# The last chunk's gate cut into thirds, and small idle matmuls in the first routing round

## The chip, the cores and the metric

The kernel runs on one NeuronCore of a Trainium2 chip. The time of a run is the device time of one execution in microseconds; "before" is the median of six executions. A profile comes from one further execution, with its own time and its own span from the first to the last instruction.

## What is computed

A gated linear recurrence (four batches, eight heads, 768 steps, head size 48) gives x, 3072 tokens of 384 numbers. Then a mixture of eight experts with balanced assignment: all token and expert pairs are gone through by falling logit, and a pair is taken when the token is still free and the expert has fewer than 384 tokens.

```python
for t in range(S):
    state = f[:, :, t, :, None] * state + np.einsum('bhd,bhe->bhde', k[:, :, t], v[:, :, t])
    y[:, :, t] = np.einsum('bhd,bhde->bhe', q[:, :, t], state)
...
logits = x @ w_gate                       # 3072 x 8
order = np.argsort(-logits.flatten())
for idx in order:
    tok, e = (int(idx) // E, int(idx) % E)
    if assigned[tok] >= 0 or counts[e] >= cap:
        continue
    assigned[tok] = e
    counts[e] += 1
...
for e in range(E):
    mask = assigned == e
    h = np.maximum(x[mask] @ w1[e], 0.0)  # 384 x 1024
    out[mask] = h @ w2[e]                 # 1024 x 384
```

## The kernel before

**Attention.** The 24 chunks (128 steps of one batch each) go through a pipeline of six stages; `attention(first, last)` runs its steps. In each step the parts of FILLING, FULL or LAST (lines 403 to 415) are issued in that order, each for the chunk whose stage is due. PE, DVE, ACT and POOL run what they are given in exactly the order in which the program issues it (`manual_schedule`), and SP issues loads. The last steps use LAST, in which only the end of the last chunks is left.

The end of a chunk: `values` and `queries` make x in two PSUM banks, which are copied to SBUF (line 355; for the last chunk one by ACT, one by DVE) and stored to DRAM by a DMA on ACT's queue. One step later `transposed` (line 360) turns x by three 128x128 transposes into one PSUM bank X, `x_copy` (367) copies X to xT on DVE in one instruction, `gate` (371) multiplies xT with the gate's weights, three blocks of 128 rows for each of two token halves, into columns D to D+E of the same bank, and `to_logits` (383) copies the result into `logits`.

Small pieces of DVE work for the routing are kept in the deque `small` and issued in the part `beside`: two in a step, one in a step of LAST. Six are queued before the last five steps: the five of `part(0, NCH - 1)` (line 670: row maximum `best`, `choice`, keys `over`, `masked`, `pick`) and `at_steps(0, NCH - 1)` (679), which compares the keys of 20 of the 24 columns with the first digit's 16 thresholds into `above`. The last four columns come with the last chunks and are done after the pipeline (lines 1176 to 1179). In the last step `counts_so_far` (379) calls `counted` (687): 20 small matmuls that count the tokens of those 20 columns over each threshold, and a DVE subtraction into `need`, what is still wanted.

**Routing.** `assign_and_run` finds the experts in rounds. Each round searches, for every expert, a threshold by five digits of 16 steps. In the first round (and two digits of the second) this is `digit_alone` (759): for each 8 columns DVE compares keys to thresholds (`reached`), PE adds the counts of the columns in 128x8 matmuls (24, or 4 for the first digit, whose other 20 are in `need`), DVE compares (`fills`) and reduces (`filled`), and one tiny matmul with `unit` gives the digit to all partitions, which the next digit's compare reads. Later rounds use `digit_beside` with expert matmuls from `pe_work` placed between. `assign` (842) counts the tokens over the found level (`sums`, a matmul with `ones`), marks them and lowers `places`.

Then `expert_list` numbers the tokens of the expert that is full: `index` loads the expert's number to SP, which starts the load of w1; `tokens` has POOL gather the rows of x in three indirect DMAs and starts the load of w2. `ffn` gives the expert's pieces to `pe_work`: three turns (transposes of gathered rows), 24 up matmuls, 24 down matmuls. In the first round `pe_work` is empty.

**Idle matmuls.** `idle_turns(n, nothing)` (124) issues n matmuls of `ones` (128x128) with `idle` (128x384, both BF16) into a bank that nobody reads. There are 19 and 12 at the start, three and a few more in the pipeline, one between the pieces of the first expert list (line 1126), 13 behind it (1133), and two in each of the second round's first two digits (776).

PSUM has eight banks: in attention six in turn under the tag "bank" and two under "sum", later three "r", three "H", one "O" (in which idle matmuls write) and `last_O`.

Of the kernel before, what the change touches and what calls it, by code (L numbers as in the profile page):

```python
# [26 lines left out]
def kernel(  # L27
# [60 lines left out]
    def ps(name, tag="bank"):  # L88
        return banks.tile([128, 512], FP32, name=name, tag=tag, bufs=BANKS[tag])
# [31 lines left out]
    k_bufs = [kept([128, H, DP], FP32, f"kg{i}") for i in range(NB)]  # L121
    a_bufs = [kept([128, 2, HP, 128], FP32, f"am{i}") for i in range(NB)]

    def idle_turns(n, nothing):

        for _ in range(n):
            nc.tensor.matmul(out=nothing[:, 0:CAP], lhsT=ones[:], rhs=idle[:], start=True,  # L127
                             stop=True)

    def constants():  # L130
# [209 lines left out]
    def queries(G):  # L340
        b, c, Y = G["b"], G["c"], G["Y"]
        G["x"] = x = work.tile([128, D], FP32, name="x", tag="x", bufs=3)
        if G["R"] is not None:
            for hp in range(HP):
                for j in range(2):
                    for par in range(2):
                        rows = slice(DP * par, DP * par + DH)
                        nc.tensor.matmul(
                            out=Y[par][HC * j:HC * j + HC, DH * hp:DH * hp + DH],
                            lhsT=G["qT"][rows, hp, HC * j:HC * j + HC],  # L350
                            rhs=G["R"][rows, hp, :],
                            start=False, stop=True, skip_group_check=True)
        for par in range(2):
            copy = nc.vector.tensor_copy if par and G["i"] == len(chunks) - 1 else nc.scalar.copy
            copy(out=x[:].rearrange("t (a r d) -> t r a d", r=2, d=DH)[:, par],
                 in_=Y[par][:, 0:HP * DH].rearrange("t (a d) -> t a d", d=DH))
        row = S * b + C * c
        nc.scalar.dma_start(out=xd[row:row + C, :], in_=x[:])

    def transposed(G):  # L360
        X = ps("X")
        for d in range(DC):
            nc.tensor.transpose(out=X[:, 128 * d:128 * d + 128],
                                in_=G["x"][:, 128 * d:128 * d + 128], identity=ident[:])
        G["X"] = X

    def x_copy(G, work=work):
        G["xT"] = work.tile([128, DC, 128], FP32, name="xT", tag="xT")
        nc.vector.tensor_copy(out=G["xT"][:].rearrange("p c t -> p (c t)"), in_=G["X"][:, 0:D])

    def gate(G):
        X = G["X"]
        for d in range(DC):
            for j in range(2):
                half = slice(HC * j, HC * j + HC)
                nc.tensor.matmul(out=X[half, D:D + E], lhsT=G["xT"][:, d, half], rhs=wg[:, d, :],
                                 start=(d == 0), stop=(d == DC - 1))

    def counts_so_far(G):
        if G["i"] == len(chunks) - 1:  # L380
            begun[3]()

    def to_logits(G, to=None):
        if to is None:
            to = logits[:, G["b"] * NCH + G["c"]]
        nc.vector.tensor_copy(out=to, in_=G["X"][:, D:D + E])

    chunks = [{"b": b, "c": c, "i": c * B + b} for c in range(NCH) for b in range(B)]
    AHEAD = 2
# [2 lines left out]
    def beside(G):  # L392
# [18 lines left out]
            (q_columns, 2), (k_columns, 2), (k_last, 2), (beside, 0), (clamp, -1), (queries, 4),  # L411
            (scores, 3))
    LAST = ((scores, 3),) + FIRST + ((x_copy, 5), (k_copy, 2), (values, 4), (queries, 4),
                                     (counts_so_far, 5), (gate, 5), (to_logits, 5),
                                     (beside, 5))

    small, small_pe = deque(), deque()
# [1 line left out]
    def attention(first, last):  # L419
        for step in range(first, last):  # L420
            if step + AHEAD < len(chunks):
                load(chunks[step + AHEAD])
            for part, stage in (FILLING if step < STAGES else
                                FULL if step < len(chunks) + 2 else LAST):
                if 0 <= step - stage < len(chunks):
                    part(chunks[step - stage])
                if part is sums and small_pe:
                    small_pe.popleft()()
                if part is beside:
                    for _ in range(min(len(small), 1 if step >= len(chunks) + 2 else 2)):  # L430
                        small.popleft()()

    for G in chunks[0:AHEAD]:
# [99 lines left out]
    def by_e(t):  # L533

        return t[:].rearrange("p c e -> p e c")
# [104 lines left out]
    def begin():  # L640

        nc.vector.memset(places[:], float(CAP))
        nc.vector.memset(wanted[:], float(CAP))
        nc.vector.memset(penalty[:], 0.0)
        nc.vector.tensor_copy(out=left[:], in_=first[:])
        nc.vector.memset(taken[:], 0.0)
        nc.vector.memset(lowest[:], 0.0)
        choice, over, pick = rt([NT, E], "choice", BF16), rt([NT], "over"), rt([NT], "pick")
        above = rt([NT, NTH], "above", BF16)
        need = rt([E], "need", FP32, 1)  # L650

        def part(c0, c1):
            n = c1 - c0

            def of(t):
                return t[:].rearrange("p (b c) -> p b c", b=B)[:, :, c0:c1]

            def of_e(t):
                return t[:].rearrange("p (b c) e -> p b c e", b=B)[:, :, c0:c1]

            def over_e(t):
                return t.unsqueeze(3).to_broadcast((128, B, n, E))

            best = rt([B, n], "best0")
            masked = rt([B, n, E], "masked0", BF16)

            def keys():
                level_keys(best[:], of(over))

            return [  # L670
                lambda: reduce(best[:], of_e(logits), ALU.max),

                lambda: tt(of_e(choice), of_e(logits), over_e(best[:]), ALU.is_equal),
                keys,
                lambda: tt(masked[:], of_e(choice), first[:].unsqueeze(1).unsqueeze(1).to_broadcast(
                    (128, B, n, E)), ALU.mult),
                lambda: reduce(of(pick), masked[:], ALU.max)]

        def at_steps(c0, c1):

            n = c1 - c0
            tt(above[:].rearrange("p (b c) t -> p b c t", b=B)[:, :, c0:c1],
               over[:].rearrange("p (b c) -> p b c", b=B)[:, :, c0:c1].unsqueeze(3).to_broadcast(
                   (128, B, n, NTH)),
               digits[0][0][:].unsqueeze(1).unsqueeze(1).to_broadcast((128, B, n, NTH)), ALU.is_ge)

        def counted():

            r = ps("counted")
            cols = [c for c in range(NT) if c % NCH < NCH - 1]  # L690
            for c in cols:
                nc.tensor.matmul(out=r[0:NTH, 0:E], lhsT=above[:, c, :], rhs=choice[:, c, :],
                                 start=(c == cols[0]), stop=(c == cols[-1]))
            tt(need[0:NTH, :], wanted[0:NTH, :], r[0:NTH, 0:E], ALU.subtract)

        return (choice, over, pick, counted, above, need), part, at_steps

    def assign_and_run(begun=None, also=None, again=None, exact=None):
# [60 lines left out]
        def digit_alone(above, parts, choice, unit, counted=None, turns=(0, 0)):  # L759

            some(pe_work, turns[0])
            r = bank("cnt", "r")
            cols = [c for c in range(NT) if not counted or c % NCH == NCH - 1]
            for c in cols:
                if c % 8 == 0 and not counted:
                    parts(c, c + 8)
                nc.tensor.matmul(out=r[0:NTH, 0:E], lhsT=above[:, c, :], rhs=choice[:, c, :],
                                 start=(c == cols[0]), stop=(c == cols[-1]))
            fills = rt([E], "fills")
            tt(fills[0:NTH, :], r[0:NTH, 0:E], counted[1][0:NTH, :] if counted else  # L770
               wanted[0:NTH, :], ALU.is_ge)
            filled = rt([1], "filled", BF16)
            reduce(filled[0:NTH, :], fills[0:NTH, :], ALU.max)
            if turns[1]:
                some(pe_work, turns[1])
                idle_turns(2, bank("nothing", "O"))
            digit = r[:, 128:129]
            nc.tensor.matmul(out=digit, lhsT=unit[0:NTH, :], rhs=filled[0:NTH, :], start=True,
                             stop=True)
            return digit, ALU.add  # L780
# [61 lines left out]
        def assign(choice, over, pick, slots):  # L842
# [4 lines left out]
            count = rt([E], "count", BF16)  # L847
            with nc.allow_low_precision("counts of at most 24"):
                reduce(count[:], by_e(sure), ALU.add)
            some(pe_work, slots[0])  # L850
            r = bank("sums", "r")
            nc.tensor.matmul(out=r[:, 0:E], lhsT=ones[:], rhs=count[:], start=True, stop=True)
# [323 lines left out]
    for n, piece in enumerate(part(NCH - 1, NCH)):  # L1176
        piece()
        if n == 2:
            at_steps(NCH - 1, NCH)
    in_order.__exit__(None, None, None)  # L1180
    attn.close()

# [150 lines left out]
```

## Time and profile before

| | us |
|---|---|
| median of six executions | 459.4 (458.15 to 462.03) |
| the profiled execution, its own time | 460.21 |
| its span | 458.4 |
| PE busy in the span | 437.4 (95%) |
| DVE busy | 265.7 (58%) |
| ACT busy | 139.3 (30%) |
| POOL busy | 135.5 (30%) |
| expert matmuls on PE, up (L1054, x384) and down (L1066, x192 and x192) | 132.6 + 67.0 + 66.7 |
| 74 idle matmuls, L127, PE | 19.4 |
| mean granted TensorE clock | 0.98 of full |

A line of the timeline gives start and length in us, the engine (PE a matmul, PEld its weight load, DVE, ACT, POOL, SP), the kernel's line, the operation, what it writes and reads, shapes, how many, and in brackets the idle time before and who ended it. The busy time of a matmul contains its way through the array, so a chain of matmuls issued 0.025 apart shows 0.17 for each.

### The profile page before, as it was taken

The numbers are of one execution on the slowest core, as the hardware profiler recorded it, in microseconds if no ns is written. First come the engines' busy times: TensorE is split into PE (matmuls) and PEld (weight loads), VectorE is DVE, ScalarE is ACT, GpSimd is POOL, SyncE is SP. The second block draws the span as 40 slices with busy tenths as digits, with TensorE's granted clock in tenths as the row PEclk, the third lists the DMA queues.
The fourth block names the chain that finished last, engine by engine and source line by source line (L and its number), as shares of the span: only waits on it lengthen the run. The fifth ranks groups of instructions, "written<-read, shape, count | busy, mean of one in ns | idle before, by whom it ended". The sixth has DMA issues, their size and how long they took to land. (4 is left out here: it accounts for less than half of the span.)

```text
span 458.4 us, 11902 instructions
## 1 busy us (share of the span) xinstructions
PE 437.4 (95%) x4893; PEld 293.8 (64%) x4893; DVE 265.7 (58%) x878; ACT 139.3 (30%) x322; POOL 135.5 (30%) x189
## 2 busy tenths in 40 slices
PE   8999999999999669999999999999999999999994
PEld 5788888888888535565565565565565565556552
DVE  5779977678987686647547647647637636000000
ACT  4566665566652001202212212212212212212210
POOL 1556655555551012032032033023023025101001
PEclk9999999999999859999999999999999999999999
DMA  9999998989511127082082072082082087400001
GB/s 156 184 200 206 195 190 188 192 182 181 122 38 37 37 68 261 0 305 75 6 294 80 8 287 85 2 292 75 13 292 70 17 292 242 175 19 34 0 19 39
DMA packets 118399, 59.11 MB, mean 129 GB/s; under 512 B 101664, under 2 KB 112960, under 8 KB 118336
## 3 DMA queue, kind: packets, MB, share of 16 engines
q1 hardware_dynamic: 111760, 44.06, 38.6%
q0 software_dynamic: 3072, 9.44, 6.3%
q10 hardware_dynamic: 3504, 4.77, 3.0%
q8 instruction: 40, 0.66, 0.6%
q14 instruction: 23, 0.19, 0.1%
HBM read 48.77 MB, written 9.49 MB: 127 GB/s over the span
## 5 line engine op out<-in xcount | busy, mean ns | idle before, releaser
L1054 PE MATMUL H<-xeT,w 128*128 128x384 f32 x384 | 132.6, 496 | 0.1
L1054 PEld LDWEIGHTS H<-xeT,w 128*128 128x128 f32 x384 | 69.1, 190 | 45.7 <-issue 4.0
L1066 PE MATMUL O<-w,hT 128*128 128x384 f32 x192 | 67.0, 491 | 0.0
L1066 PE MATMUL last_O<-w,hT 128*128 128x384 f32 x192 | 66.7, 491 | 0.0
L1058 ACT ACTIVATE hT<-H 128x384 f32<-128x384 f32 x64 | 31.4, 491 | 101.3 <-PE H L1054 85.3
L1066 PEld LDWEIGHTS last_O<-w,hT 128*128 128x128 f32 x192 | 35.1, 190 | 22.8 <-issue 1.9
L1066 PEld LDWEIGHTS O<-w,hT 128*128 128x128 f32 x192 | 34.9, 190 | 21.5 <-issue 1.3
L1071 POOL DMA_INDIRECT out_dram<-o,token x21 | 21.2, 1011 | 83.6 <-ACT o L1070 83.3
L324 DVE COPY_PREDICATED am<-mask,A 128x512 f32<-128x512 int32 x48 | 32.3, 727 | 18.2 <-PE A L319 18.2
L971 POOL TENSOR_TENSOR block<-past 128x72 f32<-128x72 f32 x8 | 2.4, 300 | 112.1 <-DVE at L551 100.1
L190 POOL TENSOR_TENSOR low<-g,upper 128x384 fp32r<-128x384 f32 x22 | 22.2, 1011 | 44.7 <-DVE upper L188 41.1
L1046 ACT COPY xeT<-Xe 128x384 f32<-128x384 f32 x24 | 11.4, 480 | 58.0 <-PE Xe L1043 57.7
L334 PE MATMUL Y<-v,am 128*64 128x48 f32 x768 | 27.5, 223 | 0.8 <-DVE am L324 0.8
L319 PE MATMUL A<-qT,kT 48*64 48x128 f32 x768 | 27.0, 273 | 1.0 <-issue 1.0
L334 PEld LDWEIGHTS Y<-v,am 128*64 128x64 f32 x768 | 24.8, 138 | 1.7 <-DVE am L324 1.3
L1013 POOL DMA_INDIRECT xe<-xd,token x21 | 21.4, 1021 | 10.9 <-DVE full L548 4.4
L243 POOL TENSOR_TENSOR kg<-k,ek 128x384 f32<-128x384 f32 x23 | 23.1, 1003 | 2.2 <-ACT ek L221 2.2
L319 PEld LDWEIGHTS A<-qT,kT 48*64 48x64 f32 x768 | 21.4, 133 | 2.1 <-issue 2.0
L220 ACT ACTIVATE eq<-dl 128x384 f32<-128x384 f32 x24 | 12.6, 523 | 30.2 <-DVE dl L218 30.2
L127 PE MATMUL nothing<-idle,ones 128*128 128x384 bf16 x74 | 19.4, 400 | 1.6 <-DVE ones L132 1.5
L1070 ACT COPY o<-O 128x384 f32<-128x384 f32 x12 | 5.8, 479 | 40.7 <-PE O L1066 40.7
L237 DVE TENSOR_TENSOR qg<-q,eq 128x384 f32<-128x384 f32 x24 | 17.4, 723 | 0.6 <-ACT eq L220 0.6
(223 smaller groups left out, 659.5 us busy)
## 6 DMA issues: line engine op xcount, KB each, us to landing
w<-in_moe_w_dram SPq DMA_DIRECT2D x16, 1536.0 KB, 7.1
f<-in_f_logit_dram SPq DMA_DIRECT2D x24, 192.0 KB, 4.8
q<-in_q_dram SPq DMA_DIRECT2D x24, 192.0 KB, 4.6
k<-in_k_dram SPq DMA_DIRECT2D x24, 192.0 KB, 4.7
v<-in_v_dram SPq DMA_DIRECT2D x24, 192.0 KB, 4.6
xd<-x ACTq DMA_DIRECT2D x24, 192.0 KB, 3.0
xe<-xd,token POOLq DMA_INDIRECT x21, 3.1
out_dram<-o,token POOLq DMA_INDIRECT x21, 2.6
```

The source lines that it names most:

```text
L127: nc.tensor.matmul(out=nothing[:, 0:CAP], lhsT=ones[:], rhs=idle[:], start=True, stop=True)
L190: nc.gpsimd.tensor_tensor(out=low[:], in0=g[:, :, 0:DH], in1=upper[:].bitcast(FP32), op=ALU.subtract)
L237: nc.vector.tensor_tensor(out=G["qg"][:, :, 0:DH], in0=G["q"][:], in1=G["eq"][:], op=ALU.mult)
L243: engine.tensor_tensor(out=G["kg"][:, :, 0:DH], in0=G["k"][:], in1=G["ek"][:], op=ALU.mult)
L319: nc.tensor.matmul(out=A[par][HC * j:HC * j + HC, 128 * hp:128 * hp + 128], lhsT=G["kT"][rows, hp, HC * j:HC * j + HC], rhs=G["qT"][rows, ...
L324: nc.vector.copy_predicated(am[:, par], mask[:].unsqueeze(1).to_broadcast((128, HP, 128)), A[par][:].rearrange("s (a t) -> s a t", t=128))
L334: nc.tensor.matmul(out=Y[par][HC * j:HC * j + HC, DH * hp:DH * hp + DH], lhsT=G["am"][:, par, hp, HC * j:HC * j + HC], rhs=G["v"][:, 2 * h ...
L1013: nc.gpsimd.indirect_dma_start(out=xe[:], out_offset=None, in_=xd[:, :], in_offset=bass.IndirectOffsetOnAxis(ap=token[:, i:i + 1], axis=0))
L1054: nc.tensor.matmul(out=L["H"][:, 0:CAP], lhsT=L["w1"][:, d, 128 * ft:128 * ft + 128], rhs=xT[:, d, :], start=(d == 0), stop=(d == DC - 1))
L1058: nc.scalar.activation(out=hT[:, ft, :], in_=L["H"][:, 0:CAP], func=AF.Relu)
L1066: nc.tensor.matmul(out=L["O"][:, 0:D], lhsT=hT[:, ft, 128 * i:128 * i + 128], rhs=L["w2"][:, ft, :], start=(ft == 0), stop=(ft == FC - 1))
L1071: nc.gpsimd.indirect_dma_start(out=outs[next(tiles)][:, :], out_offset=bass.IndirectOffsetOnAxis(ap=L["token"][:, i:i + 1], axis=0), in_=o ...
```

## The change

The gate of the last chunk gets a PSUM bank for each transpose and one for its result, and a copy for each third, the middle one on ACT. The counts so far move behind the gate and its logits; their subtraction moves behind the last `at_steps`. `small` gives two pieces in each step, also in LAST. `idle_turns` takes a size, and in `digit_alone` without turns of its own 12 (first digit) or 6 (others) idle matmuls of 128 columns stand ahead of the counts and 4 ahead of the digit's product; 12 stand ahead of the sums in `assign` when there is no expert work.

```diff
-    def idle_turns(n, nothing):
+    def idle_turns(n, nothing, size=CAP):
 
         for _ in range(n):
-            nc.tensor.matmul(out=nothing[:, 0:CAP], lhsT=ones[:], rhs=idle[:], start=True,
+            nc.tensor.matmul(out=nothing[:, 0:size], lhsT=ones[:], rhs=idle[:, 0:size], start=True,
                              stop=True)
...
+    def last(G):
+        return G.get("i") == len(chunks) - 1
+
     def transposed(G):
-        X = ps("X")
+
+        G["X"] = X = [ps("X") for _ in range(DC)] if last(G) else [ps("X")] * DC
         for d in range(DC):
-            nc.tensor.transpose(out=X[:, 128 * d:128 * d + 128],
+            nc.tensor.transpose(out=X[d][:, 128 * d:128 * d + 128],
                                 in_=G["x"][:, 128 * d:128 * d + 128], identity=ident[:])
-        G["X"] = X
 
     def x_copy(G, work=work):
-        G["xT"] = work.tile([128, DC, 128], FP32, name="xT", tag="xT")
-        nc.vector.tensor_copy(out=G["xT"][:].rearrange("p c t -> p (c t)"), in_=G["X"][:, 0:D])
+        if last(G):
+            G["xT"] = [work.tile([128, 128], FP32, name="xTd", tag="xTd", bufs=DC)
+                       for _ in range(DC)]
+            for d, t in enumerate(G["xT"]):
+                copy = nc.scalar.copy if d == 1 else nc.vector.tensor_copy
+                copy(out=t[:], in_=G["X"][d][:, 128 * d:128 * d + 128])
+        else:
+            xT = work.tile([128, DC, 128], FP32, name="xT", tag="xT")
+            nc.vector.tensor_copy(out=xT[:].rearrange("p c t -> p (c t)"), in_=G["X"][0][:, 0:D])
+            G["xT"] = [xT[:, d, :] for d in range(DC)]
 
     def gate(G):
-        X = G["X"]
+        G["lg"] = lg = ps("lg") if last(G) else G["X"][0]
         for d in range(DC):
             for j in range(2):
                 half = slice(HC * j, HC * j + HC)
-                nc.tensor.matmul(out=X[half, D:D + E], lhsT=G["xT"][:, d, half], rhs=wg[:, d, :],
+                nc.tensor.matmul(out=lg[half, D:D + E], lhsT=G["xT"][d][:, half], rhs=wg[:, d, :],
                                  start=(d == 0), stop=(d == DC - 1))
 
     def counts_so_far(G):
-        if G["i"] == len(chunks) - 1:
-            begun[3]()
+        if last(G):
+            G["need"] = begun[3]()
...
-                                     (counts_so_far, 5), (gate, 5), (to_logits, 5),
+                                     (gate, 5), (to_logits, 5), (counts_so_far, 5),
                                      (beside, 5))
...
                 if part is beside:
-                    for _ in range(min(len(small), 1 if step >= len(chunks) + 2 else 2)):
+                    for _ in range(min(len(small), 2)):
                         small.popleft()()
...
-            tt(need[0:NTH, :], wanted[0:NTH, :], r[0:NTH, 0:E], ALU.subtract)
+            return lambda: tt(need[0:NTH, :], wanted[0:NTH, :], r[0:NTH, 0:E], ALU.subtract)
...
             cols = [c for c in range(NT) if not counted or c % NCH == NCH - 1]
+            if not turns[1]:
+                idle_turns(12 if counted else 6, bank("nothing", "O"), 128)
             for c in cols:
...
                 idle_turns(2, bank("nothing", "O"))
+            else:
+                idle_turns(4, bank("nothing", "O"), 128)
             digit = r[:, 128:129]
...
                 reduce(count[:], by_e(sure), ALU.add)
+            if not pe_work:
+                idle_turns(12, bank("nothing", "O"), 128)
             some(pe_work, slots[0])
...
         if n == 2:
             at_steps(NCH - 1, NCH)
+            chunks[-1]["need"]()
```

More of the change, by code (lines that the diff above doesn't have):

```diff
@@ L353, in queries @@
         for par in range(2):
-            copy = nc.vector.tensor_copy if par and G["i"] == len(chunks) - 1 else nc.scalar.copy
+            copy = nc.vector.tensor_copy if par and last(G) else nc.scalar.copy
             copy(out=x[:].rearrange("t (a r d) -> t r a d", r=2, d=DH)[:, par],
@@ L385, in to_logits @@
             to = logits[:, G["b"] * NCH + G["c"]]
-        nc.vector.tensor_copy(out=to, in_=G["X"][:, D:D + E])
+        nc.vector.tensor_copy(out=to, in_=G["lg"][:, D:D + E])
     chunks = [{"b": b, "c": c, "i": c * B + b} for c in range(NCH) for b in range(B)]
```

## Prediction

> **What bounds the kernel now.** I read the sliced busy rows first, then the timeline around the only slices in which the TensorE clock dips, then a table of stretches cut at the clock's own steps, and last the timeline of the second round, which runs the same digit code at full clock.
>
> ```profile
> PE   8999999999999669999999999999999999999994
> ...
> PEclk9999999999999859999999999999999999999999
> ```
>
> One slice is 11.46 us. PE is full except in slices 13 and 14 (149 to 172 us), where the routing of the first expert runs alone: no expert product can start before its tokens are known. After that PE is busy to the end, so the kernel is bound by PE outside this stretch and by a serial DVE/PE chain inside it. The first weight load (168.24) and the gathers (171.26) are issued from this chain and move with it, so time taken off it comes off the end: from 179.04 PE is never short of work again.
>
> ```profile
> 152.94 0.52 PE L363 MATMUL X<-ident,x 128*128 128x128 f32 x3 [0.20 <-DVE x L355]
> ...
> 153.41 0.65 PE L692 MATMUL counted<-choice,above 128*16 128x8 bf16 x20
> 153.50 0.56 DVE L369 COPY xT<-X 128x384 f32<-128x384 f32 x1
> ...
> 154.11 0.52 PE L376 MATMUL X<-wg,xT 128*64 128x8 f32 x12
> 154.68 0.17 DVE L386 COPY logits<-X 128x8 f32<-128x8 f32 x1 [0.43 <-PE X L376]
> ...
> 155.53 0.23 DVE L544 TENSOR_TENSOR above<-over,steps 128x64 bf16<-128x64 f32 x1
> ...
> 155.81 0.25 PE L767 MATMUL cnt<-choice,above 128*16 128x8 bf16 x4 [1.18 <-DVE above L544]
> ...
> 156.17 0.15 DVE L544 TENSOR_TENSOR fills<-cnt,need 16x8 f32<-16x8 f32 x1
> ```
>
> This is the last chunk: transposes, one copy of all of X, the gate, the logits, then DVE steps to the first four counts. The copy's end (154.06) releases the gate (154.11); logits follow 0.57 after that.
>
> ```profile
> 152.99:156.40 3.41, 1.84 (x39) 1.45 (x40) 2.54 (x12) 0.00 (x0) 0.16 (x3) 0.99 0.16 58
> ...
> 166.64:170.05 3.41, 2.48 (x22) 0.95 (x21) 3.27 (x11) 0.00 (x0) 1.28 (x2) 0.50 0.19 26
> 170.05:173.47 3.42, 3.37 (x19) 1.50 (x19) 2.67 (x12) 0.00 (x0) 1.91 (x2) 0.51 0.97 392
> 173.47:176.88 3.41, 2.87 (x39) 1.88 (x37) 2.16 (x13) 0.48 (x1) 1.26 (x3) 1.00 0.81 239
> ```
>
> Columns: stretch, length, busy time of PE, PEld, DVE, ACT, POOL, then granted clock. The clock was half from 156.40 to 173.47, 17.07 us or five lengths of 3.41. It fell after a stretch with 1.84 us of PE, stayed down after 2.48, rose after 3.37, and was kept by 2.87.
>
> ```profile
> 160.01 0.15 DVE L544 TENSOR_TENSOR fills<-cnt,wanted 16x8 f32<-16x8 f32 x1 [0.44 <-PE cnt L767]
> ...
> 178.03 0.15 DVE L544 TENSOR_TENSOR fills<-cnt,wanted 16x8 f32<-16x8 f32 x1 [0.44 <-PE cnt L767]
> ```
>
> The first is a digit at half clock, the second one of round 2 at full clock: DVE waits 0.44 in both.
>
> **Part 1, the gate by thirds.** Taken singly, the three transposes start at 152.94, 153.08 and 153.19, and the old copy starts 0.31 after the last one. So the thirds are there at 153.25, 153.39 and 153.50. DVE copies from PSUM take 0.167 for 8 columns (L386), 0.358 for 192 (L355) and 0.558 for 384 (L369): 128 columns come to about 0.29 on that line (bounds 0.167 and 0.358). ACT takes 0.32 for 192 columns (L355), 0.20 for 4 (L253); I take 0.27. DVE copies third 0 from 153.27 to 153.56, ACT third 1 from 153.39 to 153.66 (its queue is free: the store's issue ends at 153.22), DVE third 2 from 153.50 to 153.79. The old step from copy to gate was 0.055, and the gate issues in pairs 0.058 apart, so the last four of its twelve instructions go from 153.85 to 153.93, and the logits copy follows the last one by 0.25 as before: 154.18 against 154.68, a gain of **0.50** (0.37 with the copies at 0.358, 0.63 at 0.167). Two of three waits are now hidden behind the third transpose.
>
> The counts so far leave the space between transposes and gate and stand behind the gate: 20 matmuls at 0.025 (their cadence) run 153.96 to 154.46 under the DVE chain, which needs 1.08 from logits to the end of `above`; they cost nothing as long as they end ahead of 155.3. Their subtraction (`need`, 0.15 on DVE) moves from a hole at 154.09 to behind `above`, ahead of `masked` and `pick`. Before, pick ended at 156.08 and fills started at 156.17, so DVE had only 0.08 to spare: of `need`'s 0.14 about **0.06** to 0.12 comes back. The comparison for 20 columns (`at_steps`, 0.48 on DVE) moves one step earlier, behind `pick` at 150.41; the X copy there starts at 150.83 instead of 150.65 and ends at 151.39, and its gate waits for PE until 152.22, so this is hidden with 0.8 to spare. It leaves DVE free for the first third, which otherwise would wait until 153.35. No DMA is added, and no queue is passed by one; three PSUM banks more are taken, whose last readers (the score masks) ended by 148.95.
>
> Part 1: -0.50 + 0.09 = **-0.41** (from -0.57 to -0.25).
>
> **Part 2, idle matmuls.** They are 12 ahead of the first counts, 6 ahead of each of the four others, 4 ahead of each of five digit products, 12 ahead of the sums: 68 of 128 bf16 columns. No such row exists. The 384-column idle matmul repeats every 0.163 at full and 0.320 at half clock; by columns that is 0.054 and 0.107. The bounds are the 128-column f32 transpose (0.109 apart at full clock, doubled 0.218) and the 8-column count (0.025). I take 0.054 and 0.107: same operand, same type.
>
> Each stands in PE's order, so what is behind it waits. Digit at half clock: product issued 160.41, six idle until 161.08; the first counts may start at 161.02, so eight counts (0.2) are 0.06 late, and the next eight, released at 161.29, are on time. Counts end issuing at 161.76, four idle until 162.19; the next product is released at 162.33. So nothing, at either clock. Ahead of the first counts: 154.46 + 12 x 0.054 = 155.11 against a release at 155.31: nothing at full clock; at 0.109 it would be 155.77, a loss of 0.46; at 0.107, if the clock fell earlier, 0.43. Ahead of the sums: 164.29 + 0.65 = 164.94 against 165.46: nothing; at half clock 165.57, a loss of 0.11. At 0.025 all are free. At 0.218 throughout, the digits alone would lose 0.9 each (some 4 us); the same operand's own two rows put this far off.
>
> What full clock is worth: the last count's start to fills is 0.203 at 161.74 and 0.203 at 177.83; digit product to `above` 0.198 at half, 0.211 at full. I take **0** per digit (from -0.02 to +0.02, so 0.1 either way over five digits). After the digits, sums, `before` and token products are eleven such short waits at most, also 0; the token counts end on the DVE compare (170.13, then 0.06).
>
> The Trainium skill, "TensorE: Matmul & The Clock Gate", section "Single matmul latency", gives a single matmul 20 ns more at half than at full clock for 8 columns. By it ten dependent products would gain 0.2 us more, an estimate from that page; the rows above show no such difference, and the rows decide.
>
> **Sum.** -0.41 + 0 = -0.4 us. The profiled execution took 460.21 (span 458.4 and 1.8 around it), so it would be 459.8. It stands 0.8 above the median; I put the same saving on the median: 459.4 - 0.4 = **459.0**.
>
> **Rivals.**
>
> *The clock falls ahead of the experts (slower).* At half clock the 14 idle turns of 384 columns from 170.43 last until 174.43, which both fills the stretch 170.05:173.47 and closes the gap to round 2's first counts (174.86). If the clock is held into this stretch, they take 14 x 0.163 = 2.3 us and end near 172.3 (all shifted by 0.4), and PE is bare until 174.46. A stretch over that hole holds 1.2 to 2.3 us of PE, near the 1.84 that let the clock fall. It then comes back only after a nearly full stretch. The first expert product would come at 178.64: up to 3.41 us of it at half clock cost 1.7, typically 1.3. 460.3, or 462.4 if two stretches are lost. It decides when a clock step lands between 171 and 173 us. For it: the steps lie 3.41 apart and need not lie the same in each execution. Against: the short turns in 165 to 170 shrink too, so the clock may fall at 170.05 as in the present rows and the 14 turns would warm it as now. The same page, Part 1, says that the window runs freely and that an idle one halves the clock; that speaks against shortening these turns, and the profiled steps agree with the length, 3.41 us.
>
> *The turns become the bound, or the clock isn't held.* At 0.107 to 0.109 each the twelve ahead of the first counts cost 0.46 and those ahead of the sums 0.11 to 0.14: 459.6. For it: the stretch 152.99:156.40 was the one that let the clock fall, and the added turns fill only 0.65 of it. Against: in the digits 1.04 us of each 1.92 was busy, and the turns bring it to about 1.6, or 2.87 in 3.41, as in the row that kept the clock.
>
> *More than the chain (faster).* Executions before spread from 458.15 to 462.03, and the profiled one isn't the quickest. If the slower ones start the experts at half clock and the change spares them that, the median goes to 458.15 - 0.4 = 457.7, or 457 with the far end of part 1 and 0.2 more from the clock. Against: nothing in this profile shows a cold start of the experts.
>
> **How the numbers follow.** Chances: forecast 0.52 (own range 458.4 to 459.6), clock falls 0.23, turns bind 0.10, faster 0.15. A half per cent, 2.3 us, is about what a measurement can tell from no change here: faster means under 457.1, slower over 461.7. Faster gets 0.09 from the last case and 0.02 from noise; slower 0.09 from the fallen clock (two lost stretches, or one and an unlucky median) and 0.03 from turns that cost 0.218; the rest, 0.77, is within. The range 457.3 to 461.2 leaves about 0.2 out.
>
> **What would show it.** Part 1: gate pairs apart by their copies, logits about 0.5 earlier after the first transpose (1.24 now, against 1.74), first fills about 0.4 earlier (2.8 after it, against 3.23). Part 2: clock rows of 1.00 from 152 to at least 165, and digits still 1.92 apart. Digits clearly under 1.85 would prove the zero for the clock wrong; counts released by PE's own turns and not by `above` would prove the turns' price wrong; a half clock after the first expert product would be the first rival.

## The result, and the profile after

The changed kernel takes 463.27 us (median of 20 executions, 460.58 to 464.69) against 459.38 for the kernel before (46 executions): ratio **1.0075**, 95% interval 1.0061 to 1.009. It is slower: the means (462.95 and 459.49) are 3.5 us apart, the medians 3.9. The forecast was 459.0 with a range up to 461.2.

The executions start the last chunk at different times (its first transpose came between 150.5 and 154.1 us in the profiles below), so all times here are counted from that transpose. Below, "turns" are the added idle matmuls. Times of single instructions, in us:

| from the last chunk's first transpose | before | after |
|---|---|---|
| last logits | 1.74 | 1.25 |
| first `fills` | 3.22 | 4.07 |
| from one digit's product to the next | 1.92 | 2.08 |
| `sums` | 12.52 | 14.16 |
| tokens | 17.86 | 19.55 |
| tokens to the first expert transpose | 4.91 | 5.84 |
| first expert product | 26.10 | 29.29 |
| 24 matmul records of "up" from there, to the start of the next | 8.64 | 10.61 |

From the last row on both need the same 270.7 us to the end. So the loss sits in five places: 1.34 between logits and the first fills (0.85 with the gain of 0.49 ahead of it), 0.64 in four digits, 0.17 ahead of the sums, 0.93 in the gather, and 2.5 at the first expert products.

The sliced rows of the page after, PE and its clock:

```profile
PE   8999999999999989999999999999999999999994
...
PEclk9999999999999656999999999999999999999998
```

PE is now busy through slices 13 to 15, and the clock is lower there for longer than before, not higher. From the timeline of the changed kernel, the first counts:

```profile
153.49 0.65 PE L703 MATMUL counted<-choice,above 128*16 128x8 bf16 x20
...
154.46 0.23 DVE L555 TENSOR_TENSOR above<-over,steps 128x64 bf16<-128x64 f32 x1
154.60 0.14 DVE L555 TENSOR_TENSOR need<-wanted,counted 16x8 f32<-16x8 f32 x1
...
154.80 1.34 PE L127 MATMUL nothing<-idle,ones 128*128 128x128 bf16 x12 [0.66 <-DVE need L555]
...
156.07 0.25 PE L780 MATMUL cnt<-choice,above 128*16 128x8 bf16 x4
...
156.43 0.15 DVE L555 TENSOR_TENSOR fills<-cnt,need 16x8 f32<-16x8 f32 x1 [1.36 <-PE cnt L780]
```

Without the turns the first counts would start at about 154.80 (the kernel without turns, gate_only below, starts them 2.44 after the first transpose). The twelve turns stand ahead of them, and they don't start behind the 20 counts so far: they wait 0.66 for `need`, and the counts start at 156.07.

The timeline of one later digit, after:

```profile
163.19 0.81 PE L127 MATMUL nothing<-idle,ones 128*128 128x128 bf16 x6
163.28 0.89 DVE L562 SCALAR_TENSOR_TENSOR above<-over,cnt,steps 128x128 bf16<-128x128 f32 x3 [0.17 <-PE cnt L793]
163.93 0.75 PE L780 MATMUL cnt<-choice,above 128*16 128x8 bf16 x24
164.61 0.61 PE L127 MATMUL nothing<-idle,ones 128*128 128x128 bf16 x4
164.72 0.15 DVE L555 TENSOR_TENSOR fills<-cnt,wanted 16x8 f32<-16x8 f32 x1 [0.54 <-PE cnt L780]
```

DVE waits 0.54 for the counts, 0.44 before. Stretches of the changed kernel between steps of its clock (length, busy time of PE, PEld, DVE, ACT, POOL, then the clock):

```profile
154.93:158.34 3.41, 3.41 (x51) 2.75 (x49) 1.33 (x6) 0.00 (x0) 0.16 (x3) 0.50 0.00 0
...
171.99:175.41 3.42, 3.36 (x12) 1.57 (x11) 3.14 (x15) 0.00 (x0) 2.43 (x3) 0.50 1.03 414
175.41:178.83 3.42, 2.39 (x36) 1.49 (x34) 1.25 (x8) 0.37 (x1) 0.74 (x2) 1.00 0.83 211
178.83:182.24 3.41, 3.41 (x34) 2.27 (x34) 1.76 (x7) 1.07 (x3) 0.00 (x0) 0.50 1.02 376
182.24:185.65 3.41, 3.41 (x6) 1.50 (x5) 1.31 (x7) 0.00 (x0) 0.00 (x0) 0.50 0.05 16
```

The clock was half from 154.93 to 175.41, through every digit with its turns. It rose as before with the 384-column idle matmuls, fell again at 178.83 and stayed down for 6.83 us, over the first expert products. Ahead of that fall PE had a hole, and the timeline says what it waited for:

```profile
175.98 0.75 PE L780 MATMUL cnt<-choice,above 128*16 128x8 bf16 x24
177.75 0.55 PE L1060 MATMUL Xe<-ident,xe 128*128 128x128 f32 x3 [1.02 <-DMA xe<-xd,token]
```

In the kernel before, the same transposes wait for nothing:

```profile
175.71 0.52 PE L1043 MATMUL Xe<-ident,xe 128*128 128x128 f32 x3
```

The first gather landed 5.34 us after its issue, 4.18 before. The DMA queues in 174.8 to 176.9, which is 2.4 to 4.5 us after that issue (packets, MB, share of 16 engines):

```profile
q0 software_dynamic: 129, 0.41, 66.1%
q1 hardware_dynamic: 50, 0.14, 16.5%
q8 instruction: 1, 0.02, 2.9%
```

One packet is a fetch of program code, 16 KB; 2.9% of 16 engines over 2.1 us is 0.97 us of one engine, in the midst of the gather's packets (q0). In the kernel before there is none in the same window. The load of w1 (q1) isn't what made the difference: gate_only_again below has 52 of its packets in that window and no fetch, and its first gather landed after 4.09; first12_own_bank has 25 and a fetch, and 4.97. That gave the second question for the experiments: do the turns harm by their time, or also by being instructions?

### The profile page after: what moved, and what is told of

It reads as the page before. It is cut to its first block, busy times and chain, and to the rows that moved or that the text cites. A ratio compares the mean times of both kernels' runs of the same rounds, so it can differ in the third digit from the quotient of the medians.

```text
span 463.0 us, 12040 instructions
## 1 busy us (share of the span) xinstructions
PE 446.3 (96%) x4961; PEld 300.4 (65%) x4961; DVE 266.0 (57%) x879; ACT 139.3 (30%) x323; POOL 135.8 (29%) x189
## 5 line engine op out<-in xcount | busy, mean ns | idle before, releaser
L1071 PE MATMUL H<-xeT,w 128*128 128x384 f32 x384 | 134.6, 502 | 0.0
L127 PE MATMUL nothing<-idle,ones 128*128 128x384 bf16 (+1 forms) x142 | 28.6, 355 | 2.3 <-DVE ones L132 1.5
L127 PEld LDWEIGHTS <-ones 128*128 128x128 bf16 x142 | 14.3, 125 | 9.8 <-issue 6.1
```

The costliest lines, as they stand in the source:

```text
L127: nc.tensor.matmul(out=nothing[:, 0:size], lhsT=ones[:], rhs=idle[:, 0:size], start=True, stop=True)
L1071: nc.tensor.matmul(out=L["H"][:, 0:CAP], lhsT=L["w1"][:, d, 128 * ft:128 * ft + 128], rhs=xT[:, d, :], start=(d == 0), stop=(d == DC - 1))
```

## The experiments

Each was compared with the kernel before on the same chip, with 6, 11 or 12 executions. Ratios have 95% intervals.

**gate_only**: the change without its turns.

```diff
-            if not turns[1]:
-                idle_turns(12 if counted else 6, bank("nothing", "O"), 128)
...
-            else:
-                idle_turns(4, bank("nothing", "O"), 128)
...
-            if not pe_work:
-                idle_turns(12, bank("nothing", "O"), 128)
```

> The change without any of its 68 small turns: gate by thirds, counts behind the gate, and the later need stay. Theory 1 (the turns did the harm: 1.33 us since the first twelve wait for the bank that need still reads, 0.16 per digit, 0.17 ahead of the sums, and a half clock at the experts): 0.3 to 0.5 us under before, ratio 0.9990 to 0.9994, logits 1.25 us after the first X transpose starts, digits 1.92 apart again, first expert product at full clock. Theory 2 (the later order of need and at_steps, or the new banks, did the harm): ratio 1.005 or more. Theory 3 (any earlier start of the chain moves it badly against the clock's steps): ratio 1.002 to 1.006 with half clock at the first expert products.

0.9988 (0.9977 to 0.9999). Its timeline:

```profile
151.01 0.52 PE L367 MATMUL X<-ident,x 128*128 128x128 f32 x3 [0.20 <-DVE x L355]
151.35 0.51 DVE L376 COPY xTd<-X 128x128 f32<-128x128 f32 x2 [0.32 <-PE X L367]
151.46 0.27 ACT L376 COPY xTd<-X 128x128 f32<-128x128 f32 x1 [0.73 <-PE X L367]
...
152.26 0.17 DVE L397 COPY logits<-lg 128x8 f32<-128x8 f32 x1 [0.40 <-PE lg L387]
...
153.45 0.24 PE L778 MATMUL cnt<-choice,above 128*16 128x8 bf16 x4 [0.66 <-DVE need L555]
```

Logits come 1.25 after the transpose, fills 2.79 (3.22 before), digits are 1.92 apart, and the first expert product is at 25.66, 0.44 earlier than before. The gate by thirds is a gain and none of the loss; theories 2 and 3 fall. Here too the first counts are released by `need`.

**turns_only**: the kernel before with all 68 turns, the same added lines on the old gate.

> The kernel before with all 68 turns and the old gate. Here need is computed ahead of the gate, so no bank that the first twelve write is still read. Theory 1: digits 2.08 apart instead of 1.92 (4 x 0.16), sums 0.17 later, the first twelve at most 0.1 late, so 0.8 us at least and up to 3 with a half clock at the experts: ratio 1.002 to 1.007. Theory 2: ratio 0.999 to 1.001.

1.0062 (1.0042 to 1.0082). Digits 2.08, sums 0.17 later after the last digit, fills 0.18 later; first gather landing 5.06, with a code fetch 2.64 us after its issue; first expert product at 27.79, 1.69 later than before, without a second fall of the clock in this profile.

**no_first12** and **first12_own_bank**: without the first twelve turns, and with them in the bank of the counts.

```diff
-            if not turns[1]:
-                idle_turns(12 if counted else 6, bank("nothing", "O"), 128)
+            if not turns[1] and not counted:
+                idle_turns(6, bank("nothing", "O"), 128)
...
+            if not turns[1] and counted:
+                idle_turns(12, r[:, 128:256], 128)
+            elif not turns[1]:
+                idle_turns(6, bank("nothing", "O"), 128)
```

> The change without the twelve turns ahead of the first counts; all others stay. Theory 1: first fills 2.8 us after the first X transpose instead of 4.07, so 1.3 us under the change itself: ratio to before 1.003 to 1.006. If the bank wait were harmless (hidden by the DVE chain), the ratio stays at 1.0075.

1.0003 (0.9988 to 1.0019), better than expected. Fills are back at 2.79. With 24 PE instructions fewer the code fetch came 5.9 us after the first gather's issue, when that gather had landed (3.93), and the clock stayed full at the experts; the first expert product came at 26.69.

> The change with the first twelve turns writing into unused columns of the bank that the counts use, so that they don't wait for need. Theory 1 with the wait as the cost: they start about 0.7 us earlier, right behind the 20 counts so far, and end at or before the release of the first counts at full clock (12 x 0.055 = 0.66), within 0.7 us of it at half clock: ratio 1.004 to 1.0065, 0.6 to 1.3 us under the change. If the twelve turns' own length is the cost, no more than 0.3 us under the change.

1.0065 (1.0043 to 1.0088): the time is at the edge of what was expected, but what it was expected from failed. The turns were released by `need` again, in another bank. Both banks belong to the routing's new pool, and it seems to be the pool as a whole that waits for the last reader of the old one; that is read from these two banks and from gate_only, where the counts themselves wait for `need`. The clock was still full here, and the wait and the turns cost 0.77 (fills at 3.56 instead of 2.79).

**first12_old_bank**: the same twelve issued ahead of the new pool.

```diff
     attention(ALL - 5, ALL)
     assert not small
+    idle_turns(12, ps("nothing", "sum"), 128)
...
-            if not turns[1]:
-                idle_turns(12 if counted else 6, bank("nothing", "O"), 128)
+            if not turns[1] and not counted:
+                idle_turns(6, bank("nothing", "O"), 128)
```

> The change with its first twelve turns issued ahead of the routing's PSUM pool, into a bank of attention's pool that was read long before. If the wait for need was the cost and not the turns' length: turns start right behind the 20 counts so far, first fills 2.8 to 2.9 us after the first X transpose (4.07 in the change, 3.56 with the counts' own bank); 1.2 us less than the change: ratio 1.003 to 1.0055 with the fetch still in the gather. If the length counts: fills at 3.3 to 3.5.

1.0036 (1.0016 to 1.0057). Fills at 2.96: without the wait, twelve turns at full clock cost 0.17 (2.79 without them). The clock stayed full up to the end of the third digit in this profile, which gives a direct comparison in its PE timeline:

```profile
154.14 0.16 PE L793 MATMUL cnt<-filled,unit 16*128 16x1 bf16 x1 [0.17 <-DVE filled L565]
...
156.06 0.16 PE L793 MATMUL cnt<-filled,unit 16*128 16x1 bf16 x1
156.15 0.51 PE L127 MATMUL nothing<-idle,ones 128*128 128x128 bf16 x6
...
157.98 0.16 PE L793 MATMUL cnt<-filled,unit 16*128 16x1 bf16 x1
...
159.94 0.18 PE L793 MATMUL cnt<-filled,unit 16*128 16x1 bf16 x1
160.06 0.81 PE L127 MATMUL nothing<-idle,ones 128*128 128x128 bf16 x6
```

Products are 1.92 apart at full clock with turns, as at half clock without; the clock fell at 158.44, and the next steps are 1.96 and 2.09. Full clock gains a digit nothing, and turns at half clock cost it 0.16. The stretch ahead of the fall also shows that turns at full clock don't hold it:

```profile
155.03:158.44 3.41, 3.20 (x65) 2.53 (x62) 2.25 (x11) 0.00 (x0) 0.00 (x0) 1.00 0.02 5
```

PE was busy for 3.20 of 3.41 us, where 2.87 had kept the clock in the kernel before, and the clock fell at its end.

**no_digit_turns**: the change without the 6 and 4.

```diff
-            if not turns[1]:
-                idle_turns(12 if counted else 6, bank("nothing", "O"), 128)
+            if counted:
+                idle_turns(12, bank("nothing", "O"), 128)
...
-            else:
-                idle_turns(4, bank("nothing", "O"), 128)
```

> The change without the 6 and 4 turns of the digits; the twelve ahead of the first counts and of the sums stay. Digits 1.92 apart instead of 2.08 (0.64 less), sums 0.17 late as in the change. With 88 PE instructions fewer the fetch leaves the gather too (Theory A): first expert product about 26.6 us after the first X transpose, ratio 1.001 to 1.003. If only the 0.64 counts: 1.006.

1.0014 (1.0001 to 1.0028): digits 1.92, no fetch in the gather (4.91 from tokens to transposes), no second fall. The first product came at 27.24 instead of 26.6, since the first twelve, at half clock, put the fills at 4.17.

**code_moved** and **gate_code_moved**: more PE instructions in the first 40 us, so that the fetches come earlier.

```diff
-    idle_turns(19, ps("nothing", "sum"))
+    idle_turns(57, ps("nothing", "sum"), 128)
...
-    idle_turns(12, ps("nothing", "sum"))
+    idle_turns(36, ps("nothing", "sum"), 128)
...
-            idle_turns(3, ps("nothing", "sum"))
+            idle_turns(9, ps("nothing", "sum"), 128)
```

code_moved has the first of these on the change, gate_code_moved all three on gate_only.

> The change itself with the first 19 idle matmuls cut into 57 of 128 columns: 76 PE instructions more, so that the fetch comes some 76 instructions earlier, ahead of the gather. Theory A: first gather lands 4.0 to 4.2 us after issue instead of 5.34, no hole of 1.1 us ahead of the first expert transposes, no second fall of the clock; first expert product 27.7 to 27.9 us after the first X transpose (29.29 in the change); ratio 1.003 to 1.0045. Theory B: ratio stays at 1.0075 and landing near 5.

1.0042 (1.0026 to 1.0058) against 1.0075: with more turns than the change it is faster. The fetch moved to 166.2, ahead of the gather; 4.91 from tokens to transposes, no second fall, first product at 27.17, which is 2.12 earlier than in the change. Of this, 0.51 isn't the fetch: in this profile the clock was still full at the first twelve turns, and fills came at 3.56.

> gate_only with the 34 idle matmuls of 384 columns in the kernel's first 40 us cut into 102 of 128 columns: the same streaming time there, but 136 PE instructions more ahead of the routing, as many as the change adds in it. Theory A (the code fetch of 16 KB, one for 256 PE instructions, delays the gather when it falls among the gather's packets): a fetch about 2.5 to 4 us after the first gather's issue, first or second gather landing 0.5 to 1.0 us later than in gate_only (4.07 and 3.06 from issue), first expert product 0.3 to 0.8 us later after the first X transpose than 25.66; ratio 1.000 to 1.003. Theory B (the late gather comes from the turns or from chance): fetch there or not, landing stays at 4.1 and the ratio at 0.9988.

1.0094 (1.0069 to 1.0119), more than expected. A fetch fell among the gather's packets, tokens to transposes took 5.86, the first product came at 27.10 (25.66 in gate_only), and the clock fell for 3.41 us there (24 records in 9.48). That is 2.3 us of some 4.9 over gate_only. The rest isn't placed; it may be a cost of cutting the first idle matmuls. So this kernel shows the fetch by its trace, not by its time.

**tiny_turns** and **tiny_more** tell instruction from duration without touching the start: first12_old_bank with all turns of 8 columns, and then with 10 and 8 per digit instead of 6 and 4.

```diff
-    idle_turns(12, ps("nothing", "sum"), 128)
+    idle_turns(12, ps("nothing", "sum"), 8)
...
-                idle_turns(6, bank("nothing", "O"), 128)
+                idle_turns(6, bank("nothing", "O"), 8)
...
-                idle_turns(4, bank("nothing", "O"), 128)
+                idle_turns(4, bank("nothing", "O"), 8)
...
-                idle_turns(12, bank("nothing", "O"), 128)
+                idle_turns(12, bank("nothing", "O"), 8)
```

> first12_old_bank with all its 68 turns cut from 128 to 8 columns: the same 136 PE instructions in the same places, but hardly any time in front of what waits behind them. Digits 1.92 apart, first fills 2.8 us after the first X transpose, sums 1.2 after the last digit, as in gate_only. Theory A (the code fetch in the gather): fetch 2.5 to 3 us after the first gather's issue, first expert transposes 5.6 to 5.9 us after the tokens instead of 4.91, half clock at the first expert products in part of the executions: ratio 1.001 to 1.005, clearly over gate_only. Theory B (only the time of the turns counts): as gate_only, 0.9988.

> tiny_turns with 10 and 8 instead of 6 and 4 turns at each digit: 72 PE instructions more again, so the next fetch comes ahead of the gather. Theory A: gather undisturbed, first expert transposes 4.91 us after the tokens, ratio back at 0.998 to 1.0005, under tiny_turns although it has more turns. Theory B, or a cost of each turn: at or over tiny_turns.

1.001 (0.9983 to 1.0036) and 0.9993 (0.9972 to 1.0015): in time the two aren't told apart. Their traces are. In both, fills come at 2.80 and digits 1.92 apart. Expert transposes and products in tiny_turns:

```profile
176.07 0.55 PE L1060 MATMUL Xe<-ident,xe 128*128 128x128 f32 x3 [0.72 <-DMA xe<-xd,token]
...
179.79 1.01 PE L1071 MATMUL H<-xeT,w 128*128 128x384 f32 x1
```

and in tiny_more:

```profile
174.93 0.52 PE L1060 MATMUL Xe<-ident,xe 128*128 128x128 f32 x3
...
178.25 2.20 PE L1071 MATMUL H<-xeT,w 128*128 128x384 f32 x6
```

With 68 turns the fetch came 2.93 us after the gather's issue, the gather landed after 5.38, the first product came at 27.02 and the clock was half over it for 3.41 us; with 104 turns the fetch came ahead, the gather landed after 4.12, and the product came at 25.64, as in gate_only.

**gate_only_again** and **change_again**: gate_only and the change once more, on the chip of tiny_turns and tiny_more.

> The same program as gate_only, on the chip of this call: 0.998 to 0.9995, transposes 4.91 us after the tokens.

0.998 (0.996 to 0.9999); first product at 25.65.

> The change itself on the chip of this call, for a second profile: fetch again 2.5 to 3 us after the first gather's issue, transposes 5.5 to 5.9 after the tokens, first twelve turns again released by need; ratio 1.006 to 1.009. Whether the clock falls a second time may differ from the first profile.

1.0069 (1.0043 to 1.0096). Everything returned: turns released by `need`, fills at 4.17, digits 2.09, a fetch 2.8 us after the gather's issue, 5.79 to the transposes, and the clock half for 6.83 us over the first products.

Over all profiles: with a fetch 2.5 to 4 us after the first gather's issue (after, change_again, turns_only, first12_own_bank, first12_old_bank, gate_code_moved, tiny_turns) tokens to transposes took 5.47 to 5.88, and in five of the seven the clock fell over the first products. In the other seven (the kernel before, both of gate_only, no_first12 with its later fetch, code_moved, no_digit_turns, tiny_more) it took 4.91 to 5.05, and the clock never fell there. That the hole in PE's work brings the second fall is read from this; no run makes such a hole by other means.

## Why the prediction was wrong

The sum was -0.41 for the gate and 0 for the turns. The first term held; the second is the step that failed. Against gate_only the turns put the first expert product back by 3.6 us (29.29 against 25.66) and the products behind it by another 2.0.

- **The gate by thirds: right.** Copies of 0.29 and 0.27 were taken and 0.292 and 0.265 measured; logits 0.49 earlier (0.50), first fills 0.43 (0.41), and at the first expert product 0.44 arrives. `need` comes back as taken, and `at_steps` cost nothing: the last chunk's transposes come 2.88 after the ones before, as in the kernel before.
- **A turn's length: right.** 0.107 at half and 0.055 at full clock.
- **"Ahead of the first counts ... nothing at full clock": failed.** The sum let the twelve start at 154.46, behind the counts so far. Moving `need` behind `above` made it, it seems, the last reader of the old pool, and the turns waited for it: 0.77 late at full clock (first12_own_bank against gate_only, 3.56 and 2.79), 1.28 to 1.38 at half. The prediction followed the readers of the three banks that the gate takes, not what the banks that the turns write wait for.
- **"So nothing, at either clock" for the digits: failed at half clock**, 0.16 each. The sum had the six turns follow the product, and the counts the turns, without a gap. In the trace the first turn starts 0.12 behind the product, and the counts start 0.24 behind the start of the last turn, which takes 0.107; so they start 0.65 after `above` began instead of 0.41, and all 24 then run in one row of 0.025 each and end 0.1 late. Ahead of `sums`, which use the turns' own weights (`ones`), the last step is 0.107, so the gap goes with the change of weights. The four turns behind them put the product back by some 0.05 more. The sums came 0.17 late; the prediction had 0.11 for half clock.
- **What full clock is worth: right**, nothing: at full clock and at half the last count's start comes 0.203 ahead of `fills`, and the steps are 1.92. By the Trainium skill ("TensorE: Matmul & The Clock Gate", section "Single matmul latency") they would be about 1.88 at full clock, an estimate from its 20 ns for each of two products; its formula is for a full 128x128 array, and these products are smaller.
- **That the clock would be held: failed.** The prediction read PE's busy time as what the clock answers to. The stretch 154.93:158.34 had PE busy for 3.41 of 3.41 and didn't raise it; chains of short matmuls look busy in that column. The second rival had this at 459.6; it had the turns' length in it, but not the wait for `need` and not the gaps in the digits.
- **The first rival came, by another road.** It was priced for 14 idle turns ending early at full clock. They ran at half clock as before; the hole came from the late gather. Its price of 1.7 us a stretch fits: 2.0 in the first products for four of the 6.83 us.
- **Not in the sum at all:** 136 more PE instructions move the fetch of code into the gather (0.93, and 2.5 more at the first products where the clock falls over them).

Less the gate's 0.49, the five places add up to 5.1 us in the profiled execution (464.89), and to 5.1 in change_again. Without the 2.5 at the first products, where the second fall is, it is about 2.6. The mean is 3.5 slower, so not all executions lose as much there. The mean granted clock, on record for each execution, says more. The nine profiles without a second fall have 0.973 to 0.980, the five with one 0.966 to 0.973. Of the 22 executions of the changed kernel on record, the profiled one among them, 13 have 0.972 or less; of 81 of the kernel before, in the experiments, none has less than 0.973. So more than half of them probably lost at least one stretch more, though the mean doesn't say where. The 13 took 463.7 on average, the other nine 462.0, which is 2.5 above the kernel before.

gate_only is the version to keep: 0.12% and 0.2% faster than the kernel before in its two measurements, with intervals that end just under 1.

## What to carry to other kernels

Filling idle time of an engine isn't free: ask what each filler instruction waits for, what stands behind it in its engine's order, and whether a faster clock would speed up anything that ends last there. A step moved later may become the last reader of a buffer pool, and the first work in the next pool may wait for it. Added instructions also move the fetches of code; look in the DMA rows for where they land beside a transfer that the chain waits for.

## What the runs showed of the hardware

Code for PE comes in packets of 16,384 bytes, 40 in the kernel before, mostly one for every 180 to 340 records of PE and its weight loads. Over all profiles those within 25 us of the first gather's issue took 0.9 to 1.7 us each. One among a gather's packets made it land about 1.1 us later (3.93 to 4.18 without, 4.97 to 5.38 with, in the ten profiles that show the landing). The Trainium skill, "Runtime: NRT & Kernel Launch", section "Instruction fetch mechanics", gives the same block, 16 KiB for 256 instructions, and calls the cost of crossing a boundary mostly hidden. What these runs show is another cost, that of the transfer beside the fetch.

The clock fell, rose and stayed in stretches of 3.41 us. The first half clock ended in all 14 profiles in a stretch with 8 to 11 of the 384-column idle matmuls (PE busy 3.36 to 3.41); rows of 128-column ones between tiny matmuls never raised it in a digit, at 3.41 busy.
